# A long convolution with routed experts: the first part's tables outside the last stage's buffers, the second group's first stage mostly behind the first sort, and the filter loaded in channel slices among x

## The chip, the cores and the metric

The kernel runs on one core of one Trainium2 chip. The metric is device time in microseconds of one launch, from a median of several runs. On the core, TensorE (PE) multiplies matrices, VectorE (DVE), ScalarE (ACT) and GpSimd (POOL) work element by element, SyncE (SP) issues the plain DMA transfers, and POOL issues the indirect ones. Each engine has one queue that it works through in order; semaphores tie the queues together.

## The reference, cut to what matters

```python
def _attn_ref(x, h):                      # x (8, 5696, 128), h (5696, 128)
    L = 2 * S
    Xf = np.fft.rfft(x, n=L, axis=1)
    Hf = np.fft.rfft(h, n=L, axis=0)
    return np.fft.irfft(Xf * Hf[None], n=L, axis=1)[:, :S, :]

def _moe_ref(x, w_gate, w1, w2):          # x (45568, 128), 8 experts, w1 (8, 128, 1024)
    logits = x @ w_gate
    expert_idx = np.argmax(logits, axis=1)
    probs = softmax(logits); gate_w = probs[range(N), expert_idx]
    for e in range(E):
        mask = expert_idx == e
        out[mask] = gate_w[mask, None] * (np.maximum(x[mask] @ w1[e], 0) @ w2[e])
```

Each channel of each of 8 sequences is convolved, causally, with a filter as long as the sequence. Every result row is a token; it goes to the one expert with the largest logit.

## The kernel before, in words

**Convolution.** A sequence is laid out as 120 x 48 (119 x 48 and padding), and the Fourier transform is done in two factors. In the *first stage* (`phase_a`, `steps_a`) an item is four columns of one sequence, 120 x 512 numbers. Each item is loaded (`load`, L278), split into a rounded part and a rest by `cut` (a cast on ACT, L269, and a subtraction, L270, on POOL for the first group and DVE for the others), multiplied in two half-items (real and imaginary, three matmuls each, `pa`, L291), copied out of PSUM (L303, ACT for the real half and DVE for the imaginary), and stored in DRAM as `U` (L284). In the *frequency stage* (`phase_b`) U is loaded by frequency (L433), transformed along 48 (`xp`, L486), multiplied with the filter's spectrum (three DVE passes, L510 to L519, and a POOL sum, L525), and transformed back (`vp`, L541). In the *sort's stage* (`phase_c`) the last transform is made (`yp`, L714), logits, the chosen expert and the rank within it are worked out, and each token row is scattered to its place in a table sorted by expert, `SR` (indirect DMA on POOL, L627, one for 120 rows).

The 8 sequences come in three groups of 2, 3 and 3. The first group holds its frequency results in SBUF, in the tile `big`, and reads them back with transposes (`lb`, L177 by `lift`), while the others go through DRAM (`V`).

**Filter.** `phase_h` loads the filter in four transfers (L366) and transforms it in 16 slices of 8 channels: a split (L376, L377), six matmuls (L388), copies, transposes (`th`), and copies into `big` (L408). **Weights.** `weights` loads each expert's matrices, splits them in two parts (L241, L243) and stores them in DRAM as `WD`.

**Tables.** When a part's rows are ranked, `tables` (L911 to L988) turns eight counts into a list of expert tiles of 256 tokens: for each tile its first row and its expert. These are some thirty tiny DVE instructions on one partition. `begin` runs what is left of them and issues the scatters that are left.

**Experts.** `experts` loads 256 sorted rows (L1024) and the expert's weights (L1050), makes two layers (`mh`, L1081; `ma`, L1101) with a ReLU between (L1087, L1089), and scatters the result to the output (L1124).

**Order.** The order of the work is written out at build time by `run`: every stage is a generator that yields the cost of its step in nanoseconds, and `run` always takes the stream whose time is lowest, where a stream's time grows by cost divided by its share. So a small share spreads a stream's steps over more of the others' time. There are five calls:

```python
run((phase_a(g0), 1.0), (phase_h(), SHARES[4]), (consts(), 1.0), (prep, SHARES[5]), stop=(prep,))
run((phase_b(g0), 1.0), (prep, SHARES[0]))
run((chain(*[gather(pt) for pt in g0.parts]), 1.0), (phase_a(groups[1]), SHARES[1]))
run((lull, 1.0), (back, LULL[1]), until=lull)
run((experts(), 1.0), (back, SHARES[3]))
```

`back` is everything of groups two and three from the second group's frequency stage on. `gather` is the sort's stage, then `tables` and, for the first part, `begin` at once. The costs decide the order in each engine's queue alone; when an instruction runs is decided by its semaphores.

**Buffers.** Tiles come from pools. The pools `lead`, `a`, `b` and `c` are opened and closed between the calls of `run`, and the pool `sb`, which serves the rest of the kernel, is opened when `c` and `lead` are closed and so lies where they lay. Tiles with a tag in `KEEP` come from a pool that stays open; the tags `wb` and `hs` there are rings of four, used in turn by the weights' preparation, the sort's row tiles (`rt`) of the first group, and the experts.

Of the kernel before, what the change touches and what calls it, by code (L numbers as in the profile page):

```python
# [13 lines left out]
F32 = mybir.dt.float32  # L14
# [9 lines left out]
NB = 48  # L24
MB = 119
QN = 120
MP = 120
# [17 lines left out]
F3 = (False, False, False, False)  # L45
MIX = 2
LD = 4
SHARES = (0.5, 0.17, 0, 0.75, 0.998, 0.84)
GAPS = (0, 6000, 5000)
HOLD = (0, 0, 0, 0)  # L50
AHEAD = 2
# [5 lines left out]
WARM = 7  # L57
TURN = (1, 1, 1, 1)
LOGIT = (2, 2, 2, 2)
LULL = (12000, 0.448)  # L60
RARE = 3
STEP = 1065
XR = 7
REST = 8000
RATE = (0.372, 0.55, 0.31, 0.8, 0.8, 0.76)


# [1 line left out]
def conv_moe(ctx: ExitStack, tc: tile.TileContext, I, out, B, S, D, E, F, split):  # L69
    nc = tc.nc  # L70
# [14 lines left out]
    keep = pool("keep", 2)  # L85
    ps = pool("ps", 2, PSUM)
    KEEP = ("wb", "hs")

    class Space:
        stack = []  # L90
# [6 lines left out]
            self.stack.pop().close()  # L97

        def tile(self, shape, dt, tag, name, **kw):
            return (keep if tag in KEEP + ("base", "did") else self.pool).tile(shape, dt, tag=tag, name=name, **kw)  # L100

    sb = Space()
    sb.open("lead")
# [62 lines left out]
    big = sb.tile([P, QN * nb0 * K2], F32, tag="big", name="big", bufs=1)  # L166
# [47 lines left out]
    def weights():  # L214
        hf = F // 2
        raws, late = {}, []

        def load(n):
            if n >= 2 * E:
                return  # L220
            e, k = divmod(n, 2)
            raws[n] = sb.tile([P, F], F32, tag="wb", name=f"wraw{n}", bufs=4)
            if k == 0:
                nc.sync.dma_start(raws[n], I["moe_w1"][e])
            else:
                nc.sync.dma_start(
                    raws[n].rearrange("p (c d) -> p c d", d=D),
                    I["moe_w2"][e].rearrange("(c p) d -> p c d", p=P),
                )

        load(0)
        yield REST
        for n in range(2 * E):
            e, k = divmod(n, 2)
            load(n + 1)
            raw = raws.pop(n)
            for u in range(2):
                yield 1500
                sp = sb.tile([P, 2, hf], F32R, tag="hs", name=f"wsp{n}_{u}", bufs=4)
                rh = raw[:, u * hf : (u + 1) * hf]  # L240
                nc.scalar.copy(sp[:, 0, :], rh)  # L241
                eng = nc.gpsimd if state["rests"] else nc.vector
                eng.tensor_tensor(out=sp[:, 1, :], in0=rh, in1=sp[:, 0, :].bitcast(F32), op=ALU.subtract)  # L243
                yield 1500
                while late:
                    nc.sync.dma_start(*late.pop(0))
                dst = WD[2 * k + u, e * P : (e + 1) * P, :]
                late.append((dst, sp.bitcast(F32).rearrange("p a f -> p (a f)")))
        yield 1500
        while late:  # L250
            nc.sync.dma_start(*late.pop(0))

    def steps_a(gr, tag, bufs):
        g, nb = gr.g, gr.nb
        srcs = [(I["x"][gr.b0 + b], b) for b in range(nb)]
        tw = 4 * D
        items = []
        for ig in range(NB // 4):
            for src, b in srcs:
                items.append((ig, src, b))  # L260
        xts, uts, xss = {}, {}, {}
        split = A3[g]

        def cut(n):
            if not split or n >= len(items):
                return
            xt = xts.pop(n)
            xs = sb.tile([MP, 2, tw], F32R, tag="us", name=f"xc{g}_{n}", bufs=2)
            nc.scalar.copy(xs[:, 0], xt)  # L269
            getattr(nc, ALO[g]).tensor_tensor(out=xs[:, 1], in0=xt, in1=xs[:, 0].bitcast(F32), op=ALU.subtract)  # L270
            xss[n] = xs

        def load(n):
            if n >= len(items):
                return
            ig, src, b = items[n]
            xts[n] = sb.tile([MP, tw], F32, tag="xt", name=f"xt{g}_{n}", bufs=5)
            nc.sync.dma_start(xts[n], src[:, ig * tw : (ig + 1) * tw])  # L278

        banks, late = {}, []  # L280

        def flush():
            while late:
                nc.sync.dma_start(*late.pop(0))  # L284

        def transform(m):
            n, c = divmod(m, 2)
            banks[m] = ps.tile([P, 512], F32, tag="cx", name=f"pa{g}_{n}_{c}", bufs=4)
            ops = [(fcs[:, c], xts[n])] if not split else [(fcr[:, u, c], xss[n][:, v]) for u, v in PASSES]
            for k, (lhs, rhs) in enumerate(ops):  # L290
                nc.tensor.matmul(banks[m][:QN, :], lhs, rhs, start=(k == 0), stop=(k == len(ops) - 1))  # L291
            if c == 1:
                (xss if split else xts).pop(n)

        def store(m):
            n, c = divmod(m, 2)
            ig, src, b = items[n]
            if b == 0:
                uts[c] = sb.tile([QN, 4, gr.cols], F32, tag=tag, name=f"ut{g}_{ig}_{c}", bufs=bufs)
            srcv = banks.pop(m)[:QN, :].rearrange("p (i d) -> p i d", d=D)  # L300
            lo = c * NB + ig * 4
            cp = nc.scalar.copy if c == 0 else nc.vector.tensor_copy
            cp(uts[c][:, :, b * D : (b + 1) * D], srcv)  # L303
            if b == nb - 1:
                late.append((gr.U[:, lo : lo + 4, :], uts[c]))

        def start():
            for n in range(4):
                load(n)
            cut(0)  # L310

        def begin(m):
            if m % 2 == 0:
                load(m // 2 + 4)
                cut(m // 2 + 1)
            transform(m)

        return start, begin, store, flush, 2 * len(items)

    def phase_a(gr):  # L320
# [39 lines left out]
    def phase_h():  # L360
        W = 8
        nd = D // W
        ht = big[:MP, : NB * D].rearrange("p (i d) -> p i d", d=D)
        for k in range(4):
            n = NB // 4
            nc.sync.dma_start(  # L366
                ht[:, k * n : (k + 1) * n].rearrange("p i d -> p (i d)"), I["h"][:, k * n * D : (k + 1) * n * D]
            )
        ucs, banks, hcs = {}, {}, {}

        def cut(n):
            if n >= nd:
                return
            hcs[n] = sb.tile([MP, 2, NB, W], F32R, tag="hc", name=f"hc{n}", bufs=2)
            src = ht[:, :, n * W : (n + 1) * W]
            nc.scalar.copy(hcs[n][:, 0], src)  # L376
            nc.gpsimd.tensor_tensor(out=hcs[n][:, 1], in0=src, in1=hcs[n][:, 0].bitcast(F32), op=ALU.subtract)  # L377

        yield 8000
        cut(0)  # L380
        for n in range(nd + 2):
            cut(n + 1)
            if n < nd:
                hc = hcs.pop(n).rearrange("p v i d -> p v (i d)")
                for c in range(2):
                    banks[c] = ps.tile([P, 512], F32, tag="mh", name=f"ph{n}_{c}", bufs=2)
                    for k, (u, v) in enumerate(PASSES):
                        nc.tensor.matmul(  # L388
                            banks[c][:QN, : NB * W], fcr[:, u, c], hc[:, v], start=(k == 0), stop=(k == 2)
                        )  # L390
            if 1 <= n <= nd:
                uc = ucs.pop(n - 1).rearrange("p c i d -> p (c i) d")
                for k in range(2):
                    tb = ps.tile([P, 4, QN], F32, tag="mx" if k else "ma", name=f"th{n}_{k}", bufs=1)
                    for d in range(4):
                        flip(tb[:K2, d], uc[:, :, 4 * k + d], QN)
                    banks[2 + k] = tb
            yield 2000
            if n < nd:
                ucs[n] = sb.tile([QN, 2, NB, W], F32, tag="uc", name=f"uc{n}", bufs=2)  # L400
                for c in range(2):
                    cp = nc.scalar.copy if c == 0 else nc.vector.tensor_copy
                    cp(ucs[n][:, c], banks[c][:QN, : NB * W].rearrange("p (i d) -> p i d", d=W))
            if 1 <= n <= nd:
                for k in range(2):
                    cp = nc.scalar.copy if k == 0 else nc.vector.tensor_copy
                    d0 = (n - 1) * W + 4 * k
                    cp(uht[:, :, d0 : d0 + 4], banks[2 + k][:K2].rearrange("p d q -> p q d"))  # L408
# [502 lines left out]
    def tables(pt):  # L911
        g, NT, base = pt.s, pt.nt, state["base"]
        last = pt is parts[-1]
        cnt = sb.tile([1, E], F32, tag="cnt", name=f"cnt{g}")
        nc.vector.tensor_tensor(out=cnt, in0=base[0:1, :E], in1=base0[0:1, :E], op=ALU.subtract)
        ci = sb.tile([1, E], I32, tag="ci", name=f"ci{g}")
# [27 lines left out]
        nc.vector.tensor_tensor(out=stp, in0=start[:, 1:], in1=start[:, :E], op=ALU.subtract)  # L944
        jr = jrow[:, :NT]
        yield
        ge = sb.tile([1, E, NT], F32, tag="yt", name=f"ge{g}")
        nc.vector.tensor_tensor(
            out=ge,
            in0=jr.rearrange("p (o j) -> p o j", o=1).broadcast_to([1, E, NT]),  # L950
# [426 lines left out]
```

## Time and profile before

| what | us |
|---|---|
| median of 3 runs | 2447.69 |
| lowest and highest | 2443.58, 2448.53 |
| the profiled execution's own time | 2441.18 |
| its span, first to last instruction | 2439.0 |
| PE busy | 2163.0 |
| DVE busy | 1556.9 |
| POOL busy | 1130.8 |
| ACT busy | 1097.0 |

A row of the timeline has the start in us, the length in us, the engine, the line in the kernel, the operation, the tiles written and read, the shapes, how many instructions are merged (x), and in brackets how long the engine was idle before it and what released it. Lengths of merged rows run from the first start to the last end. A row of stretches has the stretch, then for each engine its busy us and its number of instructions, then the clock granted to TensorE (1.00 is full), the DMA engines' busy share and GB/s. A row of groups has the shortest, median and longest instruction in ns and the first and last start.

### The profile page before, as it was taken

How to read it: one execution, taken by the hardware profiler on the slowest of the kernel's cores; microseconds unless marked ns; L12 is line 12 of the kernel's file. 1: busy time of each engine (PE TensorE's matmuls, PEld its weight loads, DVE VectorE, ACT ScalarE, POOL GpSimd, SP SyncE). 2: the span in 40 equal slices, each digit the busy share in tenths (PEclk: the TensorE clock that was granted, in tenths of full speed). 3: DMA queues.
4: the chain of work that ended last, by engine and by line, in shares of the span. 5: the costliest groups of instructions: out<-in, count | busy, mean ns of one | idle time of the engine just before them, and what ended most of it. 6: DMA issues, size and time to landing. Idle time of an engine off the chain costs nothing. (4 is left out here: it accounts for less than half of the span.)

```text
span 2439.0 us, 47156 instructions
## 1 busy us (share of the span) xinstructions
PE 2163.0 (89%) x14502; PEld 1843.7 (76%) x14502; DVE 1556.9 (64%) x3753; ACT 1097.0 (45%) x2361; POOL 1130.8 (46%) x1103
## 2 busy tenths in 40 slices
PE   7889898459999888878899999787887999999997
PEld 5688665337777776766677779777776999999997
DVE  3577455459999566657888885554555555555554
ACT  4566454214344554542344445443443444444443
POOL 5456325735555165554355553555555333333332
PEclk8899899779999999988999999998888999999999
DMA  8989666489997887757787875443423333333330
GB/s 264 284 257 276 190 179 171 132 203 259 252 252 208 221 237 209 214 138 190 198 220 211 229 188 144 124 123 99 129 68 99 115 110 113 111 113 112 113 113 29
DMA packets 212109, 420.40 MB, mean 172 GB/s; under 512 B 31745, under 2 KB 130871, under 8 KB 211856
## 3 DMA queue, kind: packets, MB, share of 16 engines
q1 hardware_dynamic: 187920, 370.27, 54.1%
q0 software_dynamic: 23936, 47.09, 6.5%
q8 instruction: 118, 1.93, 0.3%
q14 instruction: 135, 1.11, 0.2%
HBM read 578.32 MB, written 154.27 MB: 300 GB/s over the span
## 5 line engine op out<-in xcount | busy, mean ns | idle before, releaser
L1089 DVE SCALAR_TENSOR_TENSOR hs<-mh,hs 128x512 fp32r<-128x512 f32 x728 | 502.2, 691 | 473.2 <-ACT hs L1087 431.5
L1081 PE MATMUL mh<-xtb,wb 128*128 128x256 f32 x4368 | 716.2, 300 | 24.7 <-DVE hs L1089 10.8
L1101 PE MATMUL ma<-hs,wb 128*128 128x256 f32 x4368 | 669.2, 289 | 18.0 <-issue 10.0
L1087 ACT ACTIVATE hs<-mh 128x512 fp32r<-128x512 f32 x728 | 435.0, 599 | 541.4 <-PE mh L1081 398.9
L1081 PEld LDWEIGHTS mh<-xtb,wb 128*128 128x128 f32 x4368 | 599.6, 193 | 103.0 <-issue 35.9
L1124 POOL DMA_INDIRECT out<-xr x364 | 362.2, 995 | 656.2 <-DVE xr L1115 542.5
L1101 PEld LDWEIGHTS ma<-hs,wb 128*128 128x128 f32 x4368 | 582.9, 194 | 19.3 <-issue 9.5
L627 POOL DMA_INDIRECT SR<-rt,pi x384 | 396.2, 1032 | 380.2 <-issue 129.4
L525 POOL TENSOR_TENSOR zt<-zt,xs 128x384 f32<-128x384 f32 (+1 forms) x280 | 293.7, 1067 | 166.4 <-DVE xs L515 109.0
L486 PE MATMUL xp<-uq,mt 96*128 96x384 f32 (+1 forms) x720 | 269.4, 472 | 41.3 <-DMA hh<-HS 39.9
L562 ACT COPY vt<-vp 96x384 f32<-96x384 f32 x240 | 114.4, 477 | 360.0 <-PE vp L541 344.3
L519 DVE TENSOR_TENSOR xs<-xp,hh 64x384 f32<-64x384 f32 (+1 forms) x360 | 214.8, 597 | 8.6 <-POOL zt L525 0.8
L510 DVE TENSOR_TENSOR zt<-xp,hh 128x384 f32<-128x384 f32 (+1 forms) x300 | 174.0, 580 | 71.9 <-PE xp L486 44.6
L291 PE MATMUL pa<-xc,fcr 120*120 120x512 f32 x576 | 173.6, 433 | 26.0 <-ACT xc L269 14.9
L541 PE MATMUL vp<-zt,mi 128*96 128x384 f32 x480 | 194.9, 487 | 0.9 <-ACT vt L562 0.9
L486 PEld LDWEIGHTS xp<-uq,mt 96*128 96x128 f32 x720 | 125.7, 201 | 63.0 <-issue 49.5
L714 PE MATMUL yp<-vr,gcr 120*120 120x384 f32 x576 | 129.8, 363 | 27.8 <-ACT ut L303 26.6
L291 PEld LDWEIGHTS pa<-xc,fcr 120*120 120x120 f32 x576 | 102.9, 195 | 61.2 <-ACT xc L269 16.2
L515 DVE SCALAR_TENSOR_TENSOR xs<-xp,hh 64x384 f32<-64x384 f32 x240 | 134.2, 559 | 4.2
L541 PEld LDWEIGHTS vp<-zt,mi 128*96 128x96 f32 x480 | 77.8, 163 | 71.5 <-issue 38.4
L714 PEld LDWEIGHTS yp<-vr,gcr 120*120 120x120 f32 x576 | 104.3, 197 | 34.2 <-ACT ut L303 31.1
L303 DVE COPY ut<-pa 120x512 f32<-120x512 f32 x96 | 65.8, 685 | 84.9 <-PE pa L291 34.8
(128 smaller groups left out, 2313.4 us busy)
## 6 DMA issues: line engine op xcount, KB each, us to landing
wb<-WD SPq DMA_DIRECT2D x728, 512.0 KB
U<-ut SPq DMA_DIRECT2D x48, 720.0 KB
uq<-U SPq DMA_DIRECT2D x60, 576.0 KB
V<-vt SPq DMA_DIRECT2D x60, 576.0 KB
vq<-V SPq DMA_DIRECT2D x48, 720.0 KB
xr<-SR SPq DMA_DIRECT2D x182, 130.0 KB
xt<-x SPq DMA_DIRECT2D x96, 240.0 KB
hh<-HS SPq DMA_DIRECT2D x120, 192.0 KB
```

Source lines behind the costliest of these rows:

```text
L291: nc.tensor.matmul(banks[m][:QN, :], lhs, rhs, start=(k == 0), stop=(k == len(ops) - 1))
L486: nc.tensor.matmul(to, mt[:, k0 + s, :], uc, start=True, stop=True)
L519: nc.vector.tensor_tensor(out=xs[to], in0=x3[at], in1=him, op=ALU.mult)
L525: eng.tensor_tensor(out=zt, in0=zt, in1=xs, op=ALU.add)
L541: nc.tensor.matmul(vp[:K2, s * cw : (s + 1) * cw], mi[:, k0 + s, :], zt[:, s].rearrange("p b d -> p (b d)"), start=True, stop=True,)
L627: s = nc.gpsimd.indirect_dma_start(out=SR[:, :], out_offset=IndirectOffsetOnAxis(ap=pi[:, b : b + 1], axis=0), in_=rt[:, b, :], in_offset= ...
L714: nc.tensor.matmul(yp[:MP, :cw], lhs, rhs, start=(m == 0), stop=(m == len(ops) - 1))
L1081: nc.tensor.matmul(hp[:, u, :], wb[:, a, f, :], xt[:, b, :], start=(n == 0), stop=(n == 2))
L1087: done = nc.scalar.activation(hs[:, 0], hp, AF.Relu)
L1089: nc.vector.scalar_tensor_tensor(out=hs[:, 1], in0=hp, scalar=0.0, in1=hs[:, 0].bitcast(F32), op0=ALU.max, op1=ALU.subtract)
L1101: nc.tensor.matmul(accs[j], wb[:, a, f, :], hs[:, b, u, :], start=(k == 0 and u == 0 and n == 0), stop=(k == NPAIR - 1 and u == 1 and n == 2),
L1124: sc = nc.gpsimd.indirect_dma_start(out=out[:, :], out_offset=IndirectOffsetOnAxis(ap=xr[:, s, D + 1 : D + 2].bitcast(I32), axis=0), in_=x ...
```

## The change

- The first half-items of x: for the first group two slices of x are asked for at the start instead of four, and the lookahead grows over the first items (`fetch`); for the other groups nothing changes.
- The filter comes in an order in which eight channels lie together, so each of its four transfers brings four whole slices; the transfers are spread 0.7 us of the order's cost apart among those of x, and the first slice's split stands at 3.5 instead of 8 us.
- The weights' first load stands 4 us of cost later, and the time up to the first split stays the same. The preparation's share in the second call is 0.56 instead of 0.5.
- The share of the second group's first stage in the third call is 0.075 instead of 0.17.
- The small tiles of the tables come from the pool that stays open. The comparison's tile (`ge`) of the first part comes from the ring `hs`.
- The lull, which sets how much of the second group's frequency stage stands ahead of the experts, is 2000 instead of 12000 ns.

```diff
-SHARES = (0.5, 0.17, 0, 0.75, 0.998, 0.84)
+SHARES = (0.56, 0.075, 0, 0.75, 0.998, 0.84)
...
-LULL = (12000, 0.448)
+LULL = (2000, 0.448)
...
-REST = 8000
+REST = 4000
...
     KEEP = ("wb", "hs")
+    KEPT = KEEP + ("base", "did", "cnt", "ci", "nt", "end", "start", "stp", "ej", "r0")
...
-            return (keep if tag in KEEP + ("base", "did") else self.pool).tile(shape, dt, tag=tag, name=name, **kw)
+            return (keep if tag in KEPT else self.pool).tile(shape, dt, tag=tag, name=name, **kw)
...
+        yield REST
         load(0)
         yield REST
...
-        banks, late = {}, []
+        banks, late, due = {}, [], [0]
+
+        def fetch(n):
+            while due[0] <= n:
+                load(due[0])
+                due[0] += 1
...
         def start():
-            for n in range(4):
-                load(n)
+            fetch(3 if g else 1)
             cut(0)
 
         def begin(m):
             if m % 2 == 0:
-                load(m // 2 + 4)
-                cut(m // 2 + 1)
+                n = m // 2
+                fetch(n + 4 if g else n + 2 + min(n, 2))
+                cut(n + 1)
             transform(m)
...
-        ht = big[:MP, : NB * D].rearrange("p (i d) -> p i d", d=D)
+        flat = big[:MP, : NB * D]
+        ht = flat.rearrange("p (n i d) -> p n i d", n=nd, d=W)
         for k in range(4):
-            n = NB // 4
-            nc.sync.dma_start(
-                ht[:, k * n : (k + 1) * n].rearrange("p i d -> p (i d)"), I["h"][:, k * n * D : (k + 1) * n * D]
-            )
+            n = NB * D // 4
+            nc.sync.dma_start(flat[:, k * n : (k + 1) * n], I["h"][:, k * n : (k + 1) * n])
+            yield 700
...
-            src = ht[:, :, n * W : (n + 1) * W]
+            src = ht[:, n]
...
-        yield 8000
+        yield 700
         cut(0)
...
-        ge = sb.tile([1, E, NT], F32, tag="yt", name=f"ge{g}")
+        ge = sb.tile([1, E, NT], F32, tag="yt" if g else "hs", name=f"ge{g}", bufs=2 if g else 4)
...
-        "h": hp.reshape(MP, NB * D),
+        "h": hp.reshape(MP, NB, D // 8, 8).transpose(0, 2, 1, 3).reshape(MP, NB * D),
```

## The prediction

> **What bounds the kernel now.** I read the page first, then the engines' busy time by stretches, then the timeline around each stage's end.
>
> ```profile
> PE 2163.0 (89%) x14502; PEld 1843.7 (76%) x14502; DVE 1556.9 (64%) x3753; ACT 1097.0 (45%) x2361; POOL 1130.8 (46%) x1103
> ...
> PE   7889898459999888878899999787887999999997
> ...
> DMA  8989666489997887757787875443423333333330
> ```
>
> TensorE is busy nearly everywhere. The slices (61 us each) show two weak places that the change touches: the start (digit 7, with DMA at 8) and the eighth and ninth slices (4 and 5), the passage from the first sort to the experts. The stretches of that passage (busy us and count of PE, its weight loads, DVE, ACT and POOL, then granted clock, DMA share, GB/s), and its timeline:
>
> ```profile
> 455.00:460.00 5.00, 2.56 (x17) 1.35 (x16) 2.30 (x17) 0.95 (x3) 3.78 (x5) 0.94 0.21 60
> ...
> 520.00:525.00 5.00, 0.00 (x0) 0.00 (x0) 0.00 (x0) 0.00 (x0) 0.00 (x0) 0.50 1.01 374
> 550.00:650.00 100.00, 99.86 (x550) 74.58 (x550) 93.72 (x173) 40.36 (x87) 56.52 (x57) 1.00 0.95 249
> ```
>
> ```profile
> 469.04 0.14 DVE L915 TENSOR_TENSOR cnt<-base,c_base 1x8 f32<-1x8 f32 x1
> 470.43 0.16 DVE L917 TENSOR_SCALAR ci<-cnt 1x8 int32<-1x8 f32 x1 [1.25 <-DVE cnt L915]
> ...
> 495.90 0.15 DVE L985 TENSOR_TENSOR did<-did,nt 1x8 f32<-1x8 f32 x1
> 496.13 0.32 SPq L425 DMA_DIRECT2D mt<-mq  x1
> ...
> 502.51 5.88 PE L486 MATMUL xp<-uq,mt 96*128 96x384 f32 x10 [39.86 <-DMA hh<-HS]
> ```
>
> ```profile
> 491.11 1.00 POOL L627 DMA_INDIRECT SR<-rt,pi  x1 [0.30 <-issue]
> ```
>
> ```profile
> 469.04:496.05 27.01, 0.00 (x0) 0.00 (x0) 6.01 (x33) 0.00 (x0) 17.90 (x18) 0.50 0.26 71
> ```
>
> The last product of the first sort's stage is over near 457. The tables of the first part then run on VectorE: 33 instructions that are busy for 6.01 us but take 27.01, each waiting about 0.55 or 1.25 us for the one before. The first load of the second group's frequency stage goes out at 496.13, 0.1 us behind the last of them (495.90 + 0.15): the tables' tiles lie where the last stage's buffers are to lie. The sort's scatters end on POOL at 492.1. TensorE does nothing from 457 to 502.5. From there DMA is full (share 1.01, later 0.95), so **the moment at which those loads start is what the passage is worth**; all below is reckoned to it.
>
> **The start.** Now five slices of x, then the whole filter, go out before the sixth slice of x:
>
> ```profile
> 20.00:25.00 5.00, 0.00 (x0) 0.00 (x0) 0.00 (x0) 0.52 (x1) 0.00 (x0) 0.75 0.96 323
> ```
>
> ```profile
> 24.48 0.62 ACT L269 CAST xc<-xt 120x512 fp32r<-120x512 f32 x1 [8.31 <-DMA xt<-x]
> ...
> 29.59 0.92 ACT L376 CAST hc<-big 120x384 fp32r<-120x384 f32 x2
> ```
>
> ```profile
> L408 DVE COPY big<-th x16: 637/644/654, 40.5 to 101.0; 96x480 f32<-96x480 f32 x16
> ```
>
> Filter work starts at 29.6 and the stage ends with it at 101.6: 16 channel slices, 4.5 us each while x runs beside them. The change moves the first filter slice in the written order from 8.0 to 3.5 us of the order's own costs, behind two and a half items of x instead of six, and its data is a quarter of the filter (720 KB), not all of it. Three slices of x and a piece of the filter are 1.4 MB, some 6 us at the 249 GB/s above, so the data is there near 8 us; the fourth slice of x, which ACT's queue has ahead of it, is behind two filter pieces, near 12. So filter work starts near 15, not 29.6, and TensorE has it to do in the idle stretch around 20 to 25. By 30 us three slices more are done, at 2.7 us each (an estimate: 72 us less some 17 items of x at the 1.65 found below, over 16 slices): 8 us. The same bytes must move in less time, and DMA stands at 8 and 9 tenths there already, so I take 7; ends 0 (all lost to DMA) and 10. The two issues of x that are put off, the first weight load (put behind 4.8 us of the order) and the filter's reads in unbroken runs I cost at nothing: the first are taken by TensorE's queue later than they land, the second has some 10 us until its split, and the third is the same 384 elements.
>
> **The weights' preparation.** The first stage's order is now 39.6 instead of 44.1 us long (3.5 or 8.0 and 18 steps of 2.0), so preparation does (39.6 x 0.84 - 8) / 6 = 4.2 of its 16 tiles there instead of 4.8; the frequency stage of 126.9 gives 126.9 x 0.56 / 6 = 11.8 instead of 10.6. It ends with the stage now; before, 0.6 tiles were left over, seen here:
>
> ```profile
> 278.51 2.52 POOL L243 TENSOR_TENSOR wsp<-wraw,wsp 128x512 fp32r<-128x512 f32 x2 [1.98 <-ACT wsp L241]
> ...
> 281.49 9.96 SPq L278 DMA_DIRECT2D xt<-x  x8
> ...
> 286.50 4.50 PE L291 MATMUL pa<-xc,fcr 120*120 120x512 f32 x9 [3.50 <-ACT xc L269]
> ```
>
> The loads of x stood on SP behind those last stores, and TensorE waited 3.5 us and then did nine matmuls instead of three before the next synthesis: 4 us gained here (0 to 6). The added 0.6 tiles, 0.9 MB and two splits on POOL and ACT, go into a stage with DMA at 0.9: 2 us lost (0 to 6).
>
> **The first sort's stage.** The second group's first stage has 72 half-items. The sort's order is 120.4 us long; at 279/0.17 a half-item all 72 fit, at 279/0.075 = 3720 only 33. So 39 of them, 19.5 items, move behind the tables in every queue: 117 matmuls, 39 casts and copies each on ACT and DVE, some 16 loads of x and 13 stores of U on SP.
>
> ```profile
> 290.81 2.22 PE L714 MATMUL yp<-hh,c_gcs 120*120 120x384 f32 x4
> ...
> 447.52 1.45 PE L714 MATMUL yp<-hh,c_gcs 120*120 120x384 f32 x4
> ```
>
> ```profile
> 290.81:447.52 156.71, 52.82 (x190) 32.61 (x189) 21.81 (x32) 18.25 (x31) 1.00 0.59 165
> ```
>
> ```profile
> 338.52 1.45 PE L714 MATMUL yp<-hh,c_gcs 120*120 120x384 f32 x4
> ...
> 343.08 1.45 PE L714 MATMUL yp<-hh,c_gcs 120*120 120x384 f32 x4
> ```
>
> Thirty steps take 156.7 us, 5.22 each; in them the pa matmuls (the second stretch row counts only these) are 52.8 us for 32 items, 1.65 an item. With 14 items, 18 x 1.65 = 29.7 us less, a step is 4.23. But some steps take 4.56 already (338.52 to 343.08), where ACT's cast of x doesn't stand ahead of the copies that the next synthesis needs; with a half-item to a step that order is the rule. Three scatters at 1.30 (1.00 and 0.30 between) set a floor of 3.9. I take 4.1, so 30 x 1.12 = 34 us; ends 20 (4.56, nothing gained beyond the good order) and 40 (3.9).
>
> **What is late next.** The other tiles of the tables and the comparison's place in the ring of four (whose last reader, a scatter, is done some 30 scatters before) cost nothing. Tables that no longer hold the loads don't free them: the loads need all of U, and U's last items now stand behind the tables on DVE. POOL's sorts (some 30 in the tail, 1.3 us each) end with the tables as before and hold nobody. One and a half items have their casts done ahead; 18 wait. Price of an item: 1.65 by its matmuls; DMA moves 240 KB in and 240 KB out:
>
> ```profile
> U<-ut SPq DMA_DIRECT2D x48, 720.0 KB
> ...
> xt<-x SPq DMA_DIRECT2D x96, 240.0 KB
> ```
>
> That is 0.49 MB, 1.5 us at the 323 GB/s above and 2.0 at the 249. I take 1.65, 29.7 us, as nothing else uses DMA then (ends 28 and 45), and 4 us until the last 1.4 MB of U has landed. The tables' 27 us I leave as they are: nearest is their own row, since TensorE and ACT will stand still beside them as they do now.
>
> **Lull, 12000 to 2000.** Two frequency steps instead of eight stand ahead of the experts. The experts then wait for two blocks of loads, not four, but six steps more (each three VectorE passes of near 0.56 us, 10 us) are left for the stage where VectorE is at 94% and DMA at 95%. Total bytes from the loads' start are the same: 0, ends -9 and +10.
>
> **Sum.** The loads start at 496.1 - 7 + 2 - 4 - 34 + 29.7 + 4 = 486.8, a gain of **9.3 us**. The profiled execution took 2441.18 (span 2439.0), 6.5 below the median of 2447.69. Against the median, which is what will be compared: 2438.4, say **2438**, 0.4% faster.
>
> **Rivals.** *The tables' chain is short.* Elsewhere, with TensorE at work, four of the same instructions take 0.68:
>
> ```profile
> 1860.89 0.68 DVE L932 TENSOR_TENSOR end<-end,nt 1x1 f32<-1x1 f32 x4
> ```
>
> At their busy time and a little, 8 us instead of 27, the 18 items start 19 us sooner: gain 28, 2420. For it: POOL scatters run in both places. Against it: the quiet around the long chain comes back. The Trainium skill, VectorE: DVE Perf Modes, The DRAIN you can't avoid, says that a semaphore behind each of a chain of VectorE instructions costs nothing extra; by that rule the chain is 8 us and the time is this rival's, and the 27.01 us row of this trace disagrees.
>
> *Slower: VectorE's queue.* Each moved item passes VectorE twice:
>
> ```profile
> L303 DVE COPY ut<-pa 120x512 f32<-120x512 f32 x96 | 65.8, 685 | 84.9 <-PE pa L291 34.8
> ```
>
> If one such pass isn't covered, an item takes 1.65 + 0.69, some 2.4 us; with sort steps of 4.56 the loads start at 496.1 - 9 - 20 + 43 + 4 = 514, 18 later: 2466. It decides from the point where an item's price passes 2.2 us at the 4.1 us step. The idle 457 to 502 is for it: what fills that gap stands behind the same chain.
>
> *It cancels.* DMA takes the start's 7 us and an item costs 2.0: 9.3 - 7 - 6 = -4, inside 0.2% (4.9 us), about what this kernel's runs can tell from no change: 2447 to 2452. That the stages' edges merely move is the same case.
>
> **Chances.** Forecast (gain 5 to 15) 0.38, short chain 0.22, cancels 0.21, slower 0.19. So faster 0.60, same 0.21, slower 0.19. Eight in ten: from 2416 (short chain and the 3.9 us step) to 2458 (about half the slower case left out). The forecast's own range is 2433 to 2443.
>
> **What would show it.** First filter cast near 15 instead of 29.6, the first stage's end near 94; first pa of the second group 3 us behind the frequency stage; synthesis steps of 4.1; tables over near 456; then about 30 us of pa with nothing else; the first mt load near 487, two xp, experts 20 us on. Wrong if the tables end early, if pa behind them runs at over 2.2 us an item, or if the first stage ends at 101 with DMA at 1.0.

## The result, and the profile after

The changed kernel is slower: 1.0104 of the time before [1.0083, 1.0124], some 25 us; the medians are 2475.9 us and 2447.8. The forecast was 2438.

Two things must be known to read what follows. The execution that was profiled with this result took 7126 us, with products of the experts at 726 ns on the mean (301 in the run used here), so the profile after is read in a further run of the same kernel, a_again below (2455.0 us in its series, ratio 1.0113; the profiled execution itself took 2466.1). And the kernel before itself took 2430 to 2438 us in three of the series below (2448 beside the result) and 2265 to 2267 in two: every ratio is against the runs of before of its own series, which I call the long series (2430 and up) and the short ones. Each of the five series ran on another chip.

The page of that further run, its slices:

```profile
PE   8799897659999888877799999878787999999997
...
DMA  8899543789999787747788884444433333333330
```

The start is as weak as before (8, 7, 9, 9 for 7, 8, 8, 9), DMA still at 8 there, and the hole of the passage is wider and less deep (7, 6, 5 in the seventh to ninth slices for 8, 4, 5). The filter's first casts and last copies, and the first hundred microseconds of both kernels (busy us and count of PE, its loads, DVE, ACT, POOL; clock; DMA share; GB/s), before first:

```profile
0.00:100.00 100.00, 81.34 (x376) 61.03 (x377) 48.87 (x72) 53.16 (x105) 51.54 (x53) 0.91 0.87 275
```

```profile
L415 DVE COPY big<-th x16: 635/642/655, 27.2 to 99.6; 96x480 f32<-96x480 f32 x16
...
L383 ACT CAST hc<-big x16: 507/517/526, 15.5 to 93.8; 120x384 fp32r<-120x384 f32 x16
...
0.00:100.00 100.00, 83.04 (x382) 62.79 (x382) 47.73 (x72) 52.26 (x105) 51.46 (x53) 0.93 0.85 268
```

Filter work starts at 15.5 as forecast, but its last copy starts at 99.6 (101.0 before), not near 94: in the same 100 us six more matmuls are done and DMA moves no more (268 GB/s for 275).

The passage, same run: syntheses of the sort, scatters, the tables' first and last instruction, then in two stretches the moved items (those of the second group's first stage that now stand behind the tables), and the first load behind them:

```profile
L721 PE MATMUL yp<-hh,c_gcs x128: 483/486/996, 275.4 to 420.0; 120*120 120x384 f32 x128
...
L634 POOL DMA_INDIRECT SR<-rt,pi x96: 992/995/1513, 311.2 to 463.2; - x96
...
436.06 0.15 DVE L922 TENSOR_TENSOR cnt<-base,c_base 1x8 f32<-1x8 f32 x1
...
443.07 0.15 DVE L992 TENSOR_TENSOR did<-did,nt 1x8 f32<-1x8 f32 x1
...
443.20:464.20 21.00, 9.85 (x26) 6.10 (x26) 6.91 (x12) 4.04 (x7) 16.42 (x16) 0.66 0.66 177
464.20:495.90 31.70, 27.24 (x81) 17.90 (x81) 17.33 (x28) 15.82 (x28) 0.00 (x0) 0.76 0.83 273
...
502.75 0.32 SPq L432 DMA_DIRECT2D mt<-mq  x1
```

The tables are over in 7 us in this execution. The 107 matmuls behind them (about 18 items) take 52.7 us, 26 of them the first 21 us, in which POOL does its last 16 scatters and TensorE is busy for 9.85. The load goes out at 502.75, not 486.8. For comparison, before:

```profile
L714 PE MATMUL yp<-hh,c_gcs x128: 485/486/996, 279.4 to 448.5; 120*120 120x384 f32 x128
```

A second profile of the changed kernel, of another long series (after_2 below), shows the same stretch with the tables caught in it:

```profile
L721 PE MATMUL yp<-hh,c_gcs x128: 483/486/996, 274.0 to 417.9; 120*120 120x384 f32 x128
...
436.27 0.23 PE L785 MATMUL gb<-oh,ones 120*128 120x54 bf16 x1 [7.16 <-DVE sm L830]
...
446.07 0.58 ACT L310 COPY ut<-pa 120x512 f32<-120x512 f32 x1 [9.91 <-remote]
...
451.69 0.15 DVE L922 TENSOR_TENSOR cnt<-base,c_base 1x8 f32<-1x8 f32 x1
...
455.18 0.16 DVE L924 TENSOR_SCALAR ci<-cnt 1x8 int32<-1x8 f32 x1 [3.34 <-issue]
...
459.14 0.99 POOL L634 DMA_INDIRECT SR<-rt,pi  x1 [0.30 <-issue]
...
468.88 0.15 DVE L992 TENSOR_TENSOR did<-did,nt 1x8 f32<-1x8 f32 x1
...
417.90:468.90 51.00, 12.57 (x55) 7.04 (x53) 15.35 (x93) 6.49 (x16) 32.12 (x33) 0.58 0.36 98
468.90:508.50 39.60, 31.67 (x107) 20.66 (x107) 24.25 (x40) 19.55 (x34) 0.00 (x0) 0.89 0.83 286
```

While the scatters last (33 in the 42 us up to 460.1), TensorE, ScalarE and VectorE stand idle for 3 to 10 us at a time, TensorE once for 14. Part of that is waiting for one another in a chain, but not all: the second table instruction starts 3.34 us after its neighbour on the same engine has ended. POOL, which hardly waits for the others there, keeps its pace of 1.3 us a scatter. Some 9 us behind the last scatter the stall is over, and from there the items take 39.6 us / (107 / 6) = 2.2 us each. The load goes out at 515.4 there.

### The profile page after: what moved, and what is told of

It reads as the page before. It is cut to its first block, busy times and chain, and to the rows that moved or that the text cites. A ratio compares the mean times of both kernels' runs of the same rounds, so it can differ in the third digit from the quotient of the medians.

```text
span 7124.2 us, 47207 instructions
## 1 busy us (share of the span) xinstructions
PE 7056.3 (99%) x14502; PEld 5399.9 (76%) x14502; DVE 1586.8 (22%) x3751; ACT 1137.9 (16%) x2361; POOL 1137.5 (16%) x1105
## 4 chain that ended last, share of the span: by engine, by line
PE 72%; issue 25%; POOL 2%; DMA 0%; DVE 0%; another core or an unknown queue 0%; POOLq 0%; SPq 0%; ACT 0%; DVEq 0%; ACTq 0%
PE mh L1088 13%; PE ma L1108 13%; PE xp L493 11%; PE vp L548 8%; PE yp L721 7%; PE pa L298 6%; PE vp L544 3%; PE mx L178 2%; PE tp L178 2%; POOL out L1131 2%; PE hp L460 1%; PE tp L761 1%; PE lb L178 1%; PE ph L395 1%; PE th L178 1%
## 5 line engine op out<-in xcount | busy, mean ns | idle before, releaser
L1088 PE MATMUL mh<-xtb,wb 128*128 128x256 f32 x4368 | 2204.2, 726 | 1.0 <-ACT xtb L1078 1.0
L1088 PEld LDWEIGHTS mh<-xtb,wb 128*128 128x128 f32 x4368 | 1882.5, 533 | 376.9 <-issue 306.5
L1108 PE MATMUL ma<-hs,wb 128*128 128x256 f32 x4368 | 2041.1, 694 | 0.0
L1108 PEld LDWEIGHTS ma<-hs,wb 128*128 128x128 f32 x4368 | 1892.6, 543 | 36.5 <-issue 8.1
L493 PE MATMUL xp<-uq,mt 96*128 96x384 f32 (+1 forms) x720 | 869.4, 1369 | 12.4 <-DMA hh<-HS 11.9
L548 PE MATMUL vp<-zt,mi 128*96 128x384 f32 x480 | 657.7, 1511 | 0.0
L298 PE MATMUL pa<-xc,fcr 120*120 120x512 f32 x576 | 514.9, 1114 | 22.5 <-DVE ut L310 22.5
L493 PEld LDWEIGHTS xp<-uq,mt 96*128 96x128 f32 x720 | 335.1, 519 | 126.1 <-issue 122.3
L721 PE MATMUL yp<-vr,gcr 120*120 120x384 f32 x576 | 380.1, 900 | 0.7 <-ACT ut L310 0.7
L544 PEld LDWEIGHTS vp<-mi,zt 128*128 128x128 f32 x480 | 206.9, 554 | 43.2 <-issue 36.0
```

Source lines behind the costliest of these rows:

```text
L493: nc.tensor.matmul(to, mt[:, k0 + s, :], uc, start=True, stop=True)
L544: nc.tensor.matmul(vp[:, o : o + K2], zt[:, s, b], mi[:, k0 + s, :], start=True, stop=True)
L548: nc.tensor.matmul(vp[:K2, s * cw : (s + 1) * cw], mi[:, k0 + s, :], zt[:, s].rearrange("p b d -> p (b d)"), start=True, stop=True,)
L721: nc.tensor.matmul(yp[:MP, :cw], lhs, rhs, start=(m == 0), stop=(m == len(ops) - 1))
L1088: nc.tensor.matmul(hp[:, u, :], wb[:, a, f, :], xt[:, b, :], start=(n == 0), stop=(n == 2))
L1108: nc.tensor.matmul(accs[j], wb[:, a, f, :], hs[:, b, u, :], start=(k == 0 and u == 0 and n == 0), stop=(k == NPAIR - 1 and u == 1 and n == 2),
```

## Experiments

Five series, each timed in five rounds; the ratio is to before in the same series.

**First series (before 2430.3): which part.** The whole change, two of its numbers put back, and its start alone:

```
a_again     the changed kernel
share17     SHARES = (0.56, 0.17, ...)             # in the changed kernel
lull12      LULL = (12000, 0.448)                  # in the changed kernel
start_only  SHARES[1] = 0.17; LULL = (12000, 0.448); KEPT = KEEP + ("base", "did"); ge in "yt"
```

> The changed kernel once more, for a profile at the ordinary clock. Against the kernel before a ratio near 1.010, some 25 us slower. Theory T (the second group's moved items stand behind the tables on VectorE, and more is lost there than the sort's stage gains): the first load of the second group's frequency stage starts some 20 to 30 us later than 496 us, with the tables still about 27 us long. Theory S (the start or the weights lose): the first frequency stage begins at 101 us or later, and the sort's stage some 20 us later than 278. Theory L (the shorter lull): those two times are as forecast (94 and 487) and the loss comes after the experts have begun.

> The changed kernel with the second group's first stage back at a share of 0.17 (all of it beside the first sort), everything else as changed. Theory T: the loss goes; ratio 0.993 to 1.000, and with the tables in the pool that stays open the loads start near 475 us, as U is complete then. Theory S or L: still 1.008 to 1.012.

> The changed kernel with the lull back at 12000. Theory L: ratio about 1.000. Theory T or S: still near 1.010, at most 0.3 points from the changed kernel.

> Of the change only the start (x, filter, weights' loads and the preparation's share of 0.56); the tables' tiles, the share of 0.17 and the lull of 12000 are those of before. Theory T or L: the forecast gain of the start, 5 to 9 us, ratio 0.996 to 0.998. Theory S: ratio 1.006 to 1.012.

Measured: 1.0113 [1.0073, 1.0152], 1.0047 [1.0013, 1.0081], 1.0159 [1.012, 1.0198], 1.001 [0.9976, 1.0045]. The start's edits move nothing that can be measured; the smaller share seems to cost the most (1.0113 against 1.0047, the intervals just touch), the tables' tiles and the lull some 0.4% at most (1.0047 against 1.001, the intervals overlap); the old lull does not help. No theory came out as put. In a_again the tables take 7 us and the first load is 6.6 us late, not 20 to 30. share17 and start_only lie between their two forecasts, and lull12 is above both of its own. share17's first load goes out at 489.6, not near 475, although the tables' tiles are kept: the last scatter ends at 486.0 there and the tables at 486.9.

**Second series (before 2266.8): parts alone, and a version for the passage.** The kernel before with `SHARES[1] = 0.075` only; before with `LULL = (2000, 0.448)` only; the changed kernel with the tables behind the moved items; and a candidate (`pi` is the small tile with the row numbers that the scatters read):

```
share075_only  SHARES = (0.5, 0.075, ...)          # in the kernel before
lull2_only     LULL = (2000, 0.448)                # in the kernel before
tables_late    KEPT + ("pi",); begin(parts[0]) after the run of gather and phase_a
cand17         SHARES[1] = 0.17; LULL = (12000, 0.448); KEPT + ("pi",)
               tables(parts[0]) two pieces to a frequency step, over six steps
```

> The kernel before with one number changed: the second group's first stage has share 0.075 beside the first sort instead of 0.17. Theory T (the moved items are what costs: they stand behind the tables on VectorE and run alone and slowly): 1.005 to 1.008 of before, the sort's stage some 24 us shorter, the second group's first load after 500. Rival (the move costs only together with the short lull or with the moved tiles): 0.998 to 1.002.

> The kernel before with the lull of 2000 instead of 12000 and nothing else. The kernel with the whole change but the share of 0.17 was 0.47% slower than before, the one with the start's edits alone 0.1%; the rest of it is the lull or the tiles of the tables. If the lull: 1.003 to 1.005 here, the experts' first product some 10 us earlier after the load, and the stretch from it to the last one some 15 us longer. If the tiles: 0.998 to 1.002.

> The changed kernel, but the tables of the first part are put behind the moved items in VectorE's queue (ahead of the second group's frequency stage), and the tile of row numbers that the scatters read (pi) lies in the kept pool too. Theory T (place in VectorE's queue): the moved items start within 3 us of the sort's last product (near 438) and run at 1.7 to 2.0 us each, so the second group's first load goes out near 475 to 480, not 503, and the ratio is 1.000 to 1.004. Rival D (the first part's scatters slow everything until they end near 464, wherever the tables stand): the items take some 2.9 each again up to 464, the first load goes out at 490 or later, ratio 1.006 to 1.010.

> The changed kernel with share 0.17 and lull 12000 as before, with pi in the kept pool, and the tables of the first part spread over the first six frequency steps of the second group. If what held the loads was the tables and then the tiles that the last scatters read, the first load goes out near 465 to 470 instead of 490 to 496, and the ratio is 0.988 to 0.992. Rival (something else that ends with the scatters, near 487, holds the loads, or the experts wait for the scatters and tables anyway): first load after 485 or experts no earlier than before, ratio 0.998 to 1.002.

Measured: 0.9954 [0.9923, 0.9985], 0.9997 [0.9983, 1.001], 0.9961 [0.9939, 0.9983], 0.9918 [0.9888, 0.9949]. The smaller share alone gains here: my expectation missed its sign. The short lull alone costs nothing. tables_late puts the items right behind the sort, yet its load goes out at 468.3, like share075_only's 468.2: place in VectorE's queue is not what sets it, at least here, where the tables take 7 us. That theory falls in this series. The candidate's load goes out earliest of all, ahead of the 465 to 470 expected:

```profile
451.89 0.32 SPq L432 DMA_DIRECT2D mt<-mq  x1
```

In the kernel with the short lull alone, which has the passage of before:

```profile
L714 PE MATMUL yp<-hh,c_gcs x128: 485/486/996, 276.5 to 440.7; 120*120 120x384 f32 x128
...
L627 POOL DMA_INDIRECT SR<-rt,pi x96: 992/997/1494, 326.9 to 482.5; - x96
...
L985 DVE TENSOR_TENSOR did<-did,nt x1: 155/155/155, 460.1 to 460.1; 1x8 f32<-1x8 f32 x1
...
L425 SPq DMA_DIRECT2D mt<-mq x6: 318/376/429, 485.4 to 526.9; - x6
```

The tables end at 460.3, 25 us ahead of the load; the load follows the last scatter (482.5 + 1.0) by 1.9 us. What held it was not the tables.

**Third series (before 2433.5): what makes a moved item dear.**

```
one_x      load(n), second group, n >= 17: xts[n] = the tile of item 16, no DMA
scat_last  tables as in the changed kernel; then sort_one(after=last copy of ut)
           and the rest of the scatters behind it; pi in KEPT
```

> The changed kernel again, beside the three below. The two series of runs so far differ in the kernel before itself (2430 us in the first, 2267 in the second; the passage from the first sort to the experts and all later sort stages ran with long waits in the first). Theory M (the sign of the change hangs on that): 1.007 to 1.015 if the kernel before takes about 2430 here, 0.993 to 0.998 if it takes about 2267. Rival (the sign is the change's own): over 1.005 either way.

> The changed kernel, but the items 17 to 35 of the second group's first stage all read the slice of x of item 16, so 19 loads of 240 KB are left out and the result differs. Theory B (DMA sets the price of a moved item: it loads 240 KB and stores twice 240 KB, 0.74 MB, 2.4 us at 300 GB/s): the items fall to 1.65 to 1.9 us each, the second group's first load goes out 10 to 15 us earlier than in after_2, ratio 0.004 to 0.006 lower. Rival D (the first part's scatters beside them set it): the first load moves by under 4 us.

> The changed kernel, but the scatters of the first part that are left when the sort's order ends (some 30) wait for the last copy of the moved items, with the row numbers' tile kept. Rival D: without scatters beside them the moved items run at under 1.9 us and the last of them ends 10 us or more earlier than in after_2. Theory B: it ends within 4 us of after_2. The whole is 10 to 30 us slower either way, since the experts wait for the scatters.

> The kernel with share 0.17, lull 12000, the row numbers' tile kept and the tables spread over the first six frequency steps, again: 0.988 to 0.996 whether the kernel before takes 2267 or 2430 here, since nothing in it stands alone on DMA; the first load 25 us or more earlier than in before. Rival (its gain, too, belongs to the one condition): over 0.998 where the kernel before takes 2430.

Measured: after_2 1.0087 [1.0055, 1.0119], one_x 1.009 [1.0059, 1.0121], scat_last 0.9993 [0.9957, 1.003], cand17_2 0.995 [0.9922, 0.9979]. The stretch behind the tables in one_x:

```profile
463.20:493.60 30.40, 28.71 (x107) 20.33 (x107) 24.73 (x40) 20.49 (x34) 0.00 (x0) 0.87 0.75 258
```

and in scat_last, with the tables ahead of it:

```profile
437.97 0.15 DVE L922 TENSOR_TENSOR cnt<-base,c_base 1x8 f32<-1x8 f32 x1
...
444.59 0.15 DVE L992 TENSOR_TENSOR did<-did,nt 1x8 f32<-1x8 f32 x1
...
444.60:484.80 40.20, 32.28 (x107) 21.23 (x107) 24.33 (x40) 19.81 (x34) 0.00 (x0) 0.86 0.83 282
```

Each theory is right in one part and wrong in another. Without the loads of x an item costs 30.4 / 17.8 = 1.7 us instead of 2.2, as theory B had it: what it waits for is DMA (in after_2's 39.6 us ScalarE's casts wait five times for x, 10.1 us in all). One item loads 240 KB and stores two results of 240 KB (U's 720 KB holds three items of one half only), 0.74 MB, and 107 / 6 of them in 39.6 us would be 332 GB/s, more than the 286 GB/s of the row, since part of x had been loaded before: the stretch has 13 loads of x and 11 stores of U, 11.3 MB. Without scatters beside them tables and items run straight on, and the last copy ends at 484.8 instead of 508.5, as rival D had it, though the price of an item (2.25) is the same, which D had at under 1.9. The whole is 0.9% faster than after_2 in its series although the experts wait for later scatters, where I had expected 10 to 30 us more.

one_x's first load goes out at 500.5 against 515.4 (5.7 us of it because its tables are over earlier, at 463.2 instead of 468.9), and its time is no better for it (1.009). Nothing follows from that: with other numbers other experts are chosen, and it works through 4440 / 24 = 185 tiles of the experts instead of 4368 / 24 = 182, with TensorE busy in their two layers for 1409.5 us instead of after_2's 1390.5.

```profile
L1091 PE MATMUL mh<-xtb,wb x4440: 274/281/988, 522.1 to 2450.3; 128*128 128x256 f32 x194
```

cand17_2 is within its range in a long series. Its first load goes out at 466.6, 29.5 us earlier than in the trace of before, its first expert product is 16.4 us earlier, and its time is 12 us shorter than before's in this series.

**Fourth series (before 2265.5): does the sign hang on the series, and what held the loads.**

```
share075_2   as share075_only
spread_nopi  cand17 with pi back among the last stage's buffers
pi_nospread  cand17 with the tables ahead of the loads, as in the changed kernel
```

> The changed kernel, beside the share alone. Where the kernel before takes about 2430: 1.007 to 1.013, as in its two series so far. Where it takes about 2267: theory M (the sign hangs on the machine's waits) 0.994 to 1.000, rival (the sign is the change's own) over 1.005.

> The kernel before with the share 0.075 alone, again. Where the kernel before takes about 2430: theory M says slower, 1.004 to 1.010, the sort's stage only 24 us shorter and the moved items over 50 us from the stage's end to the last; the rival (the share gains by itself, and the rest of the change loses) says 0.994 to 0.998 again. Where it takes about 2267: both say 0.993 to 0.998.

> The kernel with share 0.17, lull 12000 and the tables spread over the first frequency steps, but with the row numbers' tile (pi) back among the last stage's buffers. If pi holds the loads: the first load goes out only when the scatters are done (480 to 488 where before takes 2430), 15 us or more later than in cand17, and the ratio is 0.004 or more higher. If the tables held them: as cand17, first load near 467.

> The same kernel with pi kept, but the tables ahead of the loads in VectorE's queue as in the changed kernel. If pi alone held the loads: first load near 467 as in cand17, but VectorE's first copies of the second group wait for the tables; ratio within 0.002 of cand17's. If the tables held them too: first load after 485.

Measured: 0.9999 [0.998, 1.0019], 0.9934 [0.9909, 0.9959], 1.002 [1.0005, 1.0034], 0.9894 [0.9876, 0.9912]. The change that costs 0.9 to 1.1% in the long series costs nothing here, and its share alone gains in both short series; in a long one it was not timed alone. The changed kernel's passage in this series:

```profile
L721 PE MATMUL yp<-hh,c_gcs x128: 483/486/996, 272.6 to 400.3; 120*120 120x384 f32 x128
...
L922 DVE TENSOR_TENSOR cnt<-base,c_base x1: 146/146/146, 410.9 to 410.9; 1x8 f32<-1x8 f32 x1
...
417.91 0.15 DVE L992 TENSOR_TENSOR did<-did,nt 1x8 f32<-1x8 f32 x1
...
419.30:463.80 44.50, 33.92 (x107) 22.61 (x107) 22.85 (x37) 19.62 (x34) 18.56 (x18) 0.86 0.87 280
...
437.89 0.62 ACT L271 CAST xc<-xt 120x512 fp32r<-120x512 f32 x1 [4.26 <-DMA xt<-x]
...
470.73 0.32 SPq L432 DMA_DIRECT2D mt<-mq  x1
```

Here 18 scatters run beside the items without such a stall: an item costs 44.5 / 17.8 = 2.5 us, its casts wait for the loads of x, DMA is at 0.87. The two that undo one edit of the candidate each, spread_nopi first (its last scatter, its first load), then pi_nospread (tables' end, first load):

```profile
473.79 0.99 POOL L634 DMA_INDIRECT SR<-rt,pi  x1 [0.30 <-issue]
476.62 0.32 SPq L432 DMA_DIRECT2D mt<-mq  x1
```

```profile
L992 DVE TENSOR_TENSOR did<-did,nt x1: 153/153/153, 456.4 to 456.4; 1x8 f32<-1x8 f32 x1
...
L432 SPq DMA_DIRECT2D mt<-mq x7: 317/323/463, 454.7 to 511.4; - x7
```

With pi among the buffers the load waits for the last scatter, 1.8 us behind its end; with pi kept it goes out at 454.7 (467 was expected, 451.9 measured in cand17), before the tables are even done. So the tile that the scatters read held the loads, and keeping the tables' tiles without it frees nothing.

**Fifth series (before 2438.1): the lull beside the small share.** The changed kernel with the lull of 12000, and the kernel before with share 0.075 and lull 2000.

> The changed kernel with the lull of 12000. Theory L (beside the small share the short lull costs, since six more frequency steps are left for the stage in which DMA and VectorE are full): where the kernel before takes about 2266, 0.992 to 0.997, and the stretch from the experts' first product to their last is 15 to 25 us shorter than the 1753 us of the changed kernel there. Rival (the start or the tables' tiles take the gain back): 0.998 to 1.003. Where the kernel before takes about 2430: 1.010 to 1.018 again.

> The kernel before with the share 0.075 and the lull 2000, nothing else. Theory L: where the kernel before takes about 2266, 0.998 to 1.003. Rival: 0.992 to 0.996, as the share alone. Where it takes about 2430: 1.006 to 1.014 by both.

Measured: 1.0082 [1.0044, 1.0119] and 1.0053 [1.002, 1.0085], a long series, in which both theories said nearly the same: lull12_2 came out just under its range, share_lull under its. Share and lull without the rest cost 0.5% here; what takes back the share's gain in the short series stays open. The experts' first products in before, a_again and lull12_2, first and last start:

```profile
L1081 PE MATMUL mh<-xtb,wb x4368: 274/281/757, 527.7 to 2421.0; 128*128 128x256 f32 x199
```

```profile
L1088 PE MATMUL mh<-xtb,wb x4368: 274/281/988, 524.3 to 2446.4; 128*128 128x256 f32 x199
```

```profile
L1088 PE MATMUL mh<-xtb,wb x4368: 274/281/802, 545.6 to 2438.0; 128*128 128x256 f32 x199
```

From first to last 1893.3, 1922.1 and 1892.4: the short lull lets the experts start 22 us after the first load instead of 32 or 33, and their stretch is 29 us longer. In after_2 it is 14 longer, in share_lull 1. The timed ratios with the old lull (1.0159, 1.0082) and without (1.0104, 1.0113, 1.0087) don't differ on the whole.

## Why the prediction was wrong, point by point

The moment of the first load by the prediction's own terms, in us, against the executions read above. The short series has no profile of before, so after_3 is set against lull2_only, whose passage is that of before up to the first load. Rows are rounded, so a column can miss its sum by 0.1 or 0.2.

| term | forecast | a_again (long) | after_2 (long) | after_3 (short) |
|---|---|---|---|---|
| start, weights: first synthesis | -9 | -4.0 | -5.4 | -3.9 |
| sort's stage: first to last synthesis | -34 | -24.5 | -25.2 | -36.5 |
| last synthesis to the tables' end | 0 | -24.3 | +3.6 | -1.8 |
| items behind the tables | +29.7 | +52.7 | +39.5 | +45.7 |
| until U has landed | +4 | +6.8 | +6.9 | +6.9 |
| wait for scatters, in before only | 0 | 0 | 0 | -25.2 |
| first load | -9.3 | +6.6 | +19.2 | -14.7 |

**Start.** The order came as forecast (15.5) and bought little: the last copy starts at 99.6 and 97.4 against 101.0, and at 97.6 against 98.9 in the short series, and in a_again the frequency stage's first product (112.9) comes later than before's (111.6). The step that failed is "so I take 7": start_only's 1.001 [0.9976, 1.0045] is nearer to its own lower end, 0. How much start and weights bring can't be told from one execution: in the nine of the long series that have these edits the first synthesis comes between 268.8 and 282.7, against 279.4 before.

**The sort's stage.** 4.1 us a step was about right in the short series (36.5 us gained in after_3, 34 forecast) and too good in the long ones (24.5 and 25.2).

**The items' price** is the term that was most mis-sized: 1.65 by the matmuls, measured 2.2 to 2.5, and 52.7 / 17.8 = 3.0 in a_again, where scatters run beside part of them. The byte count was wrong. I set 240 KB out beside 240 KB in, but each item stores both halves, and one_x shows that DMA is what the items wait for. The prediction named 2.2 us as the point from which the slower rival decides. Its place was mistaken, though: I put the rival on VectorE's passes, and in the 44.5 us of after_3 VectorE is busy for 22.85.

**The tables.** Left at 27 us, they took 7.2 us in a_again, 7.2 in after_3, 17.3 in after_2. The short chain, a rival at 0.22, came about in two of three, but the gain went into the dearer items. It is no rule for the long series: beside scatters the tables took 21.2, 19.2 and 27.2 us there in lull12, lull12_2 and one_x, and 6.8 in scat_last, where no scatter runs beside them. In the short series they took about 7 us wherever they stand in one piece. The Trainium skill, VectorE: DVE Perf Modes, The DRAIN you can't avoid, states that a semaphore behind each of a chain of VectorE instructions costs nothing extra; the 6.8 us of scat_last agrees, the 3.34 us wait in after_2 doesn't.

**What held the loads.** "the tables' tiles lie where the last stage's buffers are to lie" was read from a gap of 0.1 us in one execution. It was a near tie there: the scatters ended 4 us earlier, and their tile pi lay among the same buffers. With 1.9 us from the last scatter to the load, as in lull2_only, they would have held the loads to 494 instead of 496.1. The prediction costed the scatters' end as holding nobody; spread_nopi and pi_nospread show that it holds the loads. (One reading of the same passage was off: the trace before has TensorE's last product ahead of the gap at 462.4, not near 457; its row says 39.86 us of idle time.)

**The lull** at 0 with ends -9 and +10 holds within what the timed runs can tell (lull2_only 0.9997); a_again is outside, with the experts' stretch 29 us longer from a start 10 us nearer to the load.

**What the moment of the first load is worth.** The prediction reckoned everything to that moment, us for us. That does not hold. In a_again the load is 6.6 us late, the first synthesis of the later groups 11 us (821.3 for 810.1), their last one 26 us (1859.2 for 1833.4), and the profiled execution took 25 us longer. after_2 loses 19 us at the load and 24 at that last synthesis. In after_3 the load is 14.7 us early and the time is the same. What takes the rest behind the load, no run shows.

So in the long series the first load comes 7 to 19 us later instead of 9 earlier, because the 24 us taken out of the sort's stage are paid back by items that take 40 to 53 us, part of them beside scatters during which the other engines stand still; what turns that into 25 us by the end stays open. In the short series the first load comes 15 us earlier and the whole is still a draw, 0.9999, against 0.9934 for the share alone. Which of the start, the kept tiles and the lull takes those 0.65% is not settled.

The version that beats both is pi_nospread: the share and lull of before, the change's other edits, and pi kept: 0.9894 [0.9876, 0.9912] in a short series; it was not timed in a long one. With the tables spread as well it is 0.9918 [0.9888, 0.9949] in the other short series, and 0.995 [0.9922, 0.9979] in a long one. That is the gain that the change was near: all of the second group's first stage beside the sort, and the loads freed.

## What to carry to other kernels

Before moving work from beside another stage to behind it, count its bytes both ways, per item, from the DMA rows; alone it costs what its transfers cost, while beside the stage DMA had room (share 0.59). When a load follows one event by 0.1 us, look for every tile that its buffers replace and for the last reader of each, since the second in line may end only 4 us earlier. And a change of 1% or less should be timed in more than one series and on more than one chip: here the same change cost 0.9 to 1.1% in three and nothing in a fourth. What an edit does to one moment in the middle is not yet its worth: follow it to the end of the trace.

## What the runs showed of the hardware

The same kernel took 2430 to 2438 us in some series and 2265 to 2267 in others. Most of the difference lies between the first and the last synthesis of the later groups, where POOL's scatters are many: 1023 us before (long, 810.1 to 1833.4) and 891 in after_3 (short, 787.6 to 1678.9). The 200 us from 1500 to 1700 of both, before first:

```profile
1500.00:1700.00 200.00, 166.21 (x1251) 149.24 (x1250) 104.44 (x367) 90.16 (x214) 102.28 (x98) 0.92 0.43 114
```

```profile
1500.00:1700.00 200.00, 196.40 (x1649) 181.79 (x1649) 141.22 (x545) 115.23 (x276) 153.59 (x148) 1.00 0.55 145
```

A third more matmuls and half as many POOL instructions again are done in the short one, with the median product of the experts at 281 ns in both, so the difference is waiting. The granted clock (0.92 against 1.00) is lower where TensorE often stands still; in the prediction's rows of before it is 0.50 with no product at all and 1.00 with TensorE busy for 99.86 of 100 us. In the passage of the long series engines stand idle up to 14 us at a time while scatters run (after_2), and in scat_last, with the scatters taken away from beside them, tables and items run on (6.8 us and 2.25 us an item). That the scatters cause the waiting in the later stages too is argued from this and not shown. Why some series have it and others not, no run shows: no chip was used in two series, so chip and series can't be told apart. The one execution of 7126 us ran with every engine's work at its usual total but TensorE's (7056 us busy instead of 2185), at a granted clock of 1.0.
